# Top-k attention and two expert layers: cosine as a shifted sine, and max and min that read PSUM

## The chip, the core and the metric

The kernel runs on one core of a Trainium2 chip. The metric is the device time of one execution in microseconds (us). Five engines have a queue each and run side by side: PE (TensorE, matmuls into PSUM; its weight loads are shown as PEld), DVE (VectorE), ACT (ScalarE), POOL (GpSimd) and SP, which issues the DMAs. An engine takes its instructions in the order in which they were written; a wait stops everything behind it on that engine.

## What is computed

```python
scores = scale * q @ k.T            # 4 batches x 8 heads, 576 x 576, head size 64
kth    = the 32nd largest of each row
attn   = softmax over scores >= kth, others 0
x      = attn @ v                   # reshaped to 2304 tokens x 512
h      = x @ w_in                   # 512 -> 2048, w_in and w_out come as 64 bit floats
x      = (h * cos(h)) @ w_out       # back to 512
# then each token goes to the expert (of 8) with the largest logit:
y      = relu(x @ w1[e]) @ w2[e]    # 512 -> 1024 -> 512, times two gate factors
```

## The kernel before

Three pieces of work follow each other and overlap.

Attention runs in 80 units: 64 "m" units of 128 query rows of two heads, and 16 "x" units of the last 64 rows of two heads side by side. A unit transposes its queries on PE, makes scores of 128 x 288 per half row and head (L551, L566), and ACT copies each half from PSUM into the tile `sc` in SBUF (L557, L571). The two halves of a row are folded: DVE takes their elementwise maximum into `up` and their minimum into `dn` (L580). Four rounds of MAX8 (L590) with a MATCH_REPLACE8 between them (L595) take the 32 largest out of `up`; one MAX8 of `dn` (L585) and a last small one (L600) give the threshold and a flag by which a general path at the end recomputes all, if the fold was not enough. POOL makes small per-row values (L604 to L609), ACT a mask (L614), POOL subtracts it (L618), ACT takes the exponential and the row sums (L621), POOL and DVE the reciprocals (L624, L627). A DVE copy (L629) spreads the reciprocals over a 128 x 128 tile `rs`, which PE transposes (L653) beside the probabilities (L641, L652), so that after the product with v (L682) DVE can scale a transposed result (L688, L692).

The first expert layer ("MoE") works on chunks of 256 tokens as soon as their attention units are done, in 72 units of 256 hidden columns: 24 matmuls (L765 to L767), an ACT copy to `hs` (L771), then cos(h) as the sine of a folded angle: POOL makes r = h/2pi + 1/4 (L773), DVE rounds it to whole turns (L775), POOL subtracts these (L777), and ACT takes the sine, in groups of up to four units because a change between the tables of sine and exponential costs a load (L787). DVE multiplies (L795), ACT and POOL split the product in two parts (L806, L808), and 12 matmuls add it to the result (L816 to L818). Weights w_in and w_out are brought from 64 bits to two 32 bit parts in the first third (L714 to L750). Each chunk ends with its routing (L833 to L911).

The second expert layer, 8 experts, follows when all tokens are routed (L1028 to L1084).

The order on each engine is made when the program is written. A class `Plan` holds every step with a cost in ns for its engine and an urgency: ten per attention unit plus an offset per kind of step from the table `ADD`. It hands each engine the most urgent step that can start, and knows which of the limited buffers are free. Six of the eight PSUM banks (`ps`) serve all scores, transposes and MoE inputs in turn; the other two hold the sums of the first expert layer. There are four places for `sc`, four for `rr` (the angle), six for `hs` and one for `dn`. What waits for what on the chip is then set by the tiles' own readers and writers, in the order written. Two engines that read one PSUM bank are put one after the other as well, which the planner's steps don't count.

Of the kernel before, what the change touches and what calls it, by code (L numbers as in the profile page):

```python
# [8 lines left out]
F32 = mybir.dt.float32  # L9
# [8 lines left out]
P = 128  # L18
# [3 lines left out]
TWO_PI = 6.2831850  # L22
LOWEST = -3.0e38
# [5 lines left out]
UP_POOL = 0  # L29
ADD = {'q': -10.1,  # L30
 's': -13.9,
# [23 lines left out]
 'rs': 1,  # L55
# [13 lines left out]
class Buf:  # L69
    """A value in one of the places of its tag; the place is picked when the first op starts."""  # L70
# [16 lines left out]
class Plan:  # L87
    """Orders the ops of all engines: takes them in program order, finds what depends on what,
    and gives each engine the most urgent op that can start."""
# [9 lines left out]
    def tag(self, name, places, loose=False, under=None):  # L99
        """`places`: (ap, area, first, last) each; `under`: tags whose last values must have left the place."""  # L100
# [158 lines left out]
def pool(n):  # L259
    return 20.0 + n * 2.357  # L260
# [7 lines left out]
def tile_topk_attention_moe_moe2(ctx, tc, q, k, v, w_in, w_out, w_gate, w_ogate, w1, w2, out):  # L268
# [45 lines left out]
    ebias = const.tile([P, 2], F32, name="ebias")  # L314
    nc.gpsimd.memset(ebias[:, 0:1], float(-EXP_OFF * 2 ** 23))
    nc.gpsimd.memset(ebias[:, 1:2], float(2 ** 20))

# [19 lines left out]
    def x2_rows(j):  # L337
        kind, b, r = tiles[j]
        if kind == "m":
# [5 lines left out]
              + N["dn"] * HALF + N["bl"] * S + 9 * P + (N["qt"] + N["rs"] + N["xt"]) * P + 4 * (TOPK + 16) + 32  # L345
# [73 lines left out]
    cut.tag("rs", N["rs"], P)  # L419
# [6 lines left out]
    attn_tags = ("sc", "kt", "qr", "vr", "kr", "ptm", "ptx", "up", "dn", "bl", "qx", "vx", "kx", "qt", "rs", "xt", "mx",  # L426
# [24 lines left out]
    B_wg, B_table, B_x2d, B_seen, B_out = (plan.fixed() for _ in range(5))  # L451
# [74 lines left out]
    def attention(u):  # L526
# [18 lines left out]
        for c in range(2):  # L545
            if kind == "m":
                ps = [plan.buf("ps"), plan.buf("ps")]
                for j in range(2):
                    def mm(j=j, c=c, o=ps[j]):
                        at = (REM if j == 0 else 0) + c * HALF  # L550
                        nc.tensor.matmul(o.ap[:, 0:HALF], qt.ap[j * D:(j + 1) * D, :],  # L551
                                         kt.ap[j * D:(j + 1) * D, at:at + HALF], start=True, stop=True)

                    plan.op({"PE": 483.0}, mm, [qt, kt], [ps[j]], prio + ADD["s"], hold=[sc])
                for j in range(2):
                    plan.op({"ACT": act(HALF, psum=True)},
                            lambda j=j, c=c, o=ps[j]: nc.scalar.activation(  # L557
                                sc.ap[:, j, c * HALF:(c + 1) * HALF], o.ap[:, 0:HALF], AF.Copy),
                            [ps[j]], [(sc, j)], prio + ADD["s"])
            else:  # L560
                o = plan.buf("ps")

                def mm(c=c, o=o):
                    at = REM + c * HALF
                    for j in range(2):
                        nc.tensor.matmul(o.ap[j * D:(j + 1) * D, 0:HALF], qt.ap[j * D:(j + 1) * D, 0:REM],  # L566
                                         kt.ap[j * D:(j + 1) * D, at:at + HALF], start=True, stop=True)

                plan.op({"PE": 540.0}, mm, [qt, kt], [o], prio + ADD["s"], hold=[sc])
                plan.op({"ACT": act(HALF, psum=True)},  # L570
                        lambda c=c, o=o: nc.scalar.activation(sc.ap[:, 0, c * HALF:(c + 1) * HALF],  # L571
# [817 lines left out]
```

## Time and profile before

| what | value |
|---|---|
| time, median of 3 runs (lowest to highest) | 1383.35 us (1379.19 to 1383.68) |
| span of the profiled execution | 1382.2 us |
| DVE busy | 988.5 us (72%) |
| PE busy | 1180.1 us (85%) |
| POOL busy | 885.2 us (64%) |
| ACT busy | 854.9 us (62%) |
| last L580, the end of the attention's top-k work | begins at 965.1 us |

The profiled execution's span is 1.15 us below the median of the runs. Busy time is a share of the whole span; the stages differ, so the stretches below are 0 to 380 us (attention, weights being narrowed, few MoE units), 380 to 968 (attention and MoE together), 968 to 1045 (MoE alone), 1045 to 1075 (change to the second layer) and from 1075 on (second layer). [...]

### The profile page before, as it was taken

How to read it: one execution, taken by the hardware profiler on the slowest of the kernel's cores; microseconds unless marked ns; L12 is line 12 of the kernel's file. 1: busy time of each engine (PE TensorE's matmuls, PEld its weight loads, DVE VectorE, ACT ScalarE, POOL GpSimd, SP SyncE). 2: the span in 40 equal slices, each digit the busy share in tenths (PEclk: the TensorE clock that was granted, in tenths of full speed). 3: DMA queues.
4: the chain of work that ended last, by engine and by line, in shares of the span. 5: the costliest groups of instructions: out<-in, count | busy, mean ns of one | idle time of the engine just before them, and what ended most of it. 6: DMA issues, size and time to landing. Idle time of an engine off the chain costs nothing.

```text
span 1382.2 us, 22655 instructions
## 1 busy us (share of the span) xinstructions
PE 1180.1 (85%) x7478; PEld 936.6 (68%) x7479; DVE 988.5 (72%) x2864; ACT 854.9 (62%) x1854; POOL 885.2 (64%) x1130
## 2 busy tenths in 40 slices
PE   3467778768898999999989898899994599999996
PEld 2334555547677668668767676767883599999995
DVE  6999999779599888999987889888335234444410
ACT  5777777767577787777766668767555244444421
POOL 6778888888666865776676657766765455555400
PEclk9655779989999989999999999999996699999998
DMA  8223323534440343323345321241557444444100
GB/s 210 76 107 113 98 67 116 182 131 162 144 139 8 111 140 105 122 92 104 96 135 152 100 78 36 89 137 46 174 184 267 166 160 158 149 156 160 58 17 23
DMA packets 95807, 164.72 MB, mean 119 GB/s; under 512 B 49850, under 2 KB 54202, under 8 KB 95680
## 3 DMA queue, kind: packets, MB, share of 16 engines
q1 hardware_dynamic: 91264, 153.71, 34.3%
q0 software_dynamic: 4416, 9.47, 2.1%
q8 instruction: 61, 1.00, 0.3%
q14 instruction: 66, 0.54, 0.1%
HBM read 146.72 MB, written 19.56 MB: 120 GB/s over the span
## 4 chain that ended last, share of the span: by engine, by line
PE 41%; DVE 29%; POOL 13%; issue 10%; ACT 6%; DMA 2%; POOLq 0%; DVEq 0%; ACTq 0%
DVE area_a L590 7%; DVE area_a L595 6%; DVE area_a L580 6%; PE bank L682 4%; PE bank L551 3%; PE bank L816 3%; PE bank L818 3%; PE bank L817 3%; PE bank L1052 2%; PE bank L1053 2%; PE bank L641 2%; PE bank L1054 2%; POOL area_a L618 2%; PE bank L765 2%; POOL area_g L777 2%
## 5 line engine op out<-in xcount | busy, mean ns | idle before, releaser
L590 DVE MAX8 area_a<-area_a 128x8 f32<-128x288 f32 x576 | 243.6, 444 | 1.1
L618 POOL TENSOR_TENSOR area_a<-area_a 128x576 f32<-128x576 f32 x144 | 195.8, 1368 | 23.0 <-ACT area_a L614 21.9
L595 DVE MATCH_REPLACE8 area_a<-area_a 128x288 f32<-128x288 f32 x432 | 187.8, 438 | 0.0
L580 DVE TENSOR_TENSOR area_a<-area_a 128x288 f32<-128x288 f32 x288 | 176.7, 639 | 14.5 <-ACT area_a L557 11.0
L765 PE MATMUL bank<-area_f,area_w 128*128 128x256 f32 x576 | 177.6, 308 | 2.3 <-ACT area_h L771 2.3
L641 PE MATMUL bank<-ident,area_a 128*128 128x128 f32 x576 | 104.5, 313 | 70.6 <-ACT area_a L621 57.8
L766 PE MATMUL bank<-area_f,area_w 128*128 128x256 f32 x576 | 163.3, 284 | 0.0
L767 PE MATMUL bank<-area_f,area_w 128*128 128x256 f32 x576 | 163.0, 283 | 0.0
L551 PE MATMUL bank<-area_a 64*128 64x288 f32 x512 | 133.3, 513 | 25.5 <-ACT area_a L541 22.5
L641 PEld LDWEIGHTS bank<-ident,area_a 128*128 128x128 f32 x576 | 73.8, 158 | 100.3 <-ACT area_a L621 78.4
L816 PE MATMUL bank<-area_l,area_f 128*128 128x512 f32 x288 | 130.4, 453 | 1.3 <-ACT area_f L806 0.6
L614 ACT ACTIVATE area_a<-area_a 128x576 bf16<-128x576 f32 x144 | 107.3, 768 | 37.5 <-POOL area_a L604 37.2
L808 POOL TENSOR_TENSOR area_f<-area_g,area_f 128x256 fp32r<-128x256 f32 x144 | 114.9, 811 | 23.7 <-ACT area_f L806 20.8
L777 POOL TENSOR_TENSOR area_g<-area_g,area_n 128x512 f32<-128x512 f32 x72 | 105.7, 1468 | 35.3 <-DVE area_a L600 14.8
L621 ACT ACTIVATE area_a<-area_a 128x576 f32<-128x576 f32 x144 | 111.2, 773 | 27.1 <-POOL area_a L618 26.2
L682 PE MATMUL bank<-area_a 128*64 128x128 f32 (+3 forms) x1600 | 123.3, 296 | 1.5 <-ACT area_a L662 1.3
L818 PE MATMUL bank<-area_l,area_f 128*128 128x512 f32 x288 | 119.7, 416 | 5.3 <-POOL area_f L808 5.0
L765 PEld LDWEIGHTS bank<-area_f,area_w 128*128 128x128 f32 x576 | 112.1, 195 | 14.2 <-issue 9.2
L682 PEld LDWEIGHTS bank<-area_a 128*64 128x64 f32 (+1 forms) x1600 | 89.8, 150 | 42.3 <-issue 18.3
L817 PE MATMUL bank<-area_l,area_f 128*128 128x512 f32 x288 | 118.2, 410 | 0.0
L766 PEld LDWEIGHTS bank<-area_f,area_w 128*128 128x128 f32 x576 | 111.8, 194 | 1.0
L767 PEld LDWEIGHTS bank<-area_f,area_w 128*128 128x128 f32 x576 | 111.0, 193 | 0.0
(197 smaller groups left out, 3005.4 us busy)
## 6 DMA issues: line engine op xcount, KB each, us to landing
area_l<-wod SPq DMA_DIRECT2D x144, 512.0 KB, 3.6
area_l<-in_moe_w_dram SPq DMA_DIRECT2D x52, 512.0 KB, 4.3
area_l<-in_moe_w_in_dram SPq DMA_DIRECT2D x16, 512.0 KB, 4.3
area_l<-in_moe_w_out_dram SPq DMA_DIRECT2D x16, 512.0 KB, 4.1
wod<-area_l SPq DMA_DIRECT2D x16, 512.0 KB, 2.6
area_n<-in_moe_w_dram SPq DMA_DIRECT2D x12, 512.0 KB, 4.9
area_a<-in_k_dram SPq DMA_DIRECT2D x32, 128.0 KB, 3.5
area_a<-in_q_dram SPq DMA_DIRECT2D x32, 128.0 KB, 3.4
```

Source lines behind the costliest of these rows:

```text
L551: nc.tensor.matmul(o.ap[:, 0:HALF], qt.ap[j * D:(j + 1) * D, :], kt.ap[j * D:(j + 1) * D, at:at + HALF], start=True, stop=True)
L580: plan.op(cost, lambda j=j, to=to, op=op, eng=eng: eng.tensor_tensor(to(), sc.ap[:, j, 0:HALF], sc.ap[:, j, HALF:S], op=op), [(sc, j)], [( ...
L590: lambda j=j, t=t: nc.vector.max(mx.ap[:, j, 8 * t:8 * t + 8], up.ap[:, j, :]),
L595: lambda j=j, t=t: nc.vector.match_replace(up.ap[:, j, :], mx.ap[:, j, 8 * t:8 * t + 8], up.ap[:, j, :], LOWEST),
L618: plan.op({"POOL": 1234.0}, lambda j=j: nc.gpsimd.tensor_tensor(sc.ap[:, j, :], sc.ap[:, j, :], bl.ap[:, j, :], op=OP.subtract), [(bl, j)] ...
L641: nc.tensor.transpose(pp.ap[:, r_ * P:(r_ + 1) * P], flat[:, at + r_ * P:at + (r_ + 1) * P], ident)
L682: nc.tensor.matmul(o.ap[j * D:(j + 1) * D, 0:w], lh, rh, start=(r_ == 0), stop=(r_ == R))
L765: nc.tensor.matmul(o, w_in_h[:, c_, fs], xh[:, c_, :], start=(c_ == 0), stop=False)
L766: nc.tensor.matmul(o, w_in_h[:, c_, fs], xl[:, c_, :], start=False, stop=False)
L767: nc.tensor.matmul(o, w_in_l[:, c_, fs], xh[:, c_, :], start=False, stop=(c_ == KC - 1))
L816: nc.tensor.matmul(acc[t].ap, gh, wr(0), start=(f == 0), stop=False)
L818: nc.tensor.matmul(acc[t].ap, gl, wr(0), start=False, stop=(f == NF - 1))
```

## The change

The angle isn't folded any more. ACT takes sin(h + pi/2) straight from `hs`, with the quarter turn as a bias that it reads from a constant tile; the POOL step, the DVE step and the POOL step ahead of it (L773, L775, L777) are gone. So that the angle stays in the range of the sine, a guard bounds |h|: PE multiplies the token chunk and the weight columns with themselves (`gram`, 72 and 64 matmuls of 128 x 128), DVE takes the largest entry of each block (13 reductions), and at the end a token norm squared over 1.60 or a weight norm squared over 1.50 sends the program to the general path.

The first halves of the scores stay in PSUM for the maximum and the minimum: of each unit ACT copies the second half (`high`) to SBUF first, DVE reads the first half (`low`) from PSUM and the second from SBUF, and ACT copies `low` to `sc` as well, with an urgency of its own, for the later steps. The number of copies is the same. A `low` bank is free when DVE and ACT have both read it.

The spread of the reciprocal sums moves from DVE to PE: the copy L629 and the tile `rs` are gone, and instead of the transpose L653 PE multiplies the column of reciprocals, read with step 0 as 64 or 128 equal weight columns, with the identity (144 matmuls for 80 transposes).

```diff
         sc = plan.buf("sc")
...
+        low = [plan.buf("ps") for _ in range(n)]
+        high = [plan.buf("ps") for _ in range(n)]
...
+        plan.op({"PE": 620.0}, lambda: scores(1, high), [qt, kt], high, prio + ADD["s"], hold=[sc])
+        plan.op({"PE": 620.0}, lambda: scores(0, low), [qt, kt], low, prio + ADD["s"], hold=[sc])
+        for j in range(n):
+            plan.op({"ACT": act(HALF, psum=True)}, lambda j=j: nc.scalar.activation(
+                sc.ap[:, j, HALF:S], high[j].ap[:, 0:HALF], AF.Copy), [high[j]], [(sc, (j, 1))], prio + ADD["s"])
...
-                plan.op(cost, lambda j=j, to=to, op=op, eng=eng: eng.tensor_tensor(
-                    to(), sc.ap[:, j, 0:HALF], sc.ap[:, j, HALF:S], op=op),
-                    [(sc, j)], [(up, j) if o_ else dns[j]], prio + ADD["top"])
+                plan.op({"DVE": vec(HALF)}, lambda j=j, to=to, op=op: nc.vector.tensor_tensor(
+                    to(), low[j].ap[:, 0:HALF], sc.ap[:, j, HALF:S], op=op),
+                    [low[j], (sc, (j, 1))], [(up, j) if o_ else dns[j]], prio + ADD["top"])
...
+        for j in range(n):
+            plan.op({"ACT": act(HALF, psum=True)}, lambda j=j: nc.scalar.activation(
+                sc.ap[:, j, 0:HALF], low[j].ap[:, 0:HALF], AF.Copy), [low[j]], [(sc, (j, 0))], prio + ADD["low"])
...
-        plan.op({"DVE": 136.0}, lambda: nc.vector.tensor_copy(
-            rs.ap.rearrange("p (h d) -> p h d", h=n),
-            sm.ap[:, 6:6 + n, None].to_broadcast([P, n, P // n])), [(sm, 6)], [rs], prio + ADD["sum"])
...
-            nc.tensor.transpose(px.ap[:, P:2 * P], rs.ap, ident)
+            for j in range(n):
+                w_ = P // n
+                nc.tensor.matmul(px.ap[j * w_:(j + 1) * w_, P:2 * P], sm.ap[:, 6 + j:7 + j].to_broadcast([P, w_]), ident,
+                                 start=True, stop=True)
...
-        plan.op({"POOL": pool_s(512)}, lambda: nc.gpsimd.tensor_scalar(
-            rr.ap, hs.ap, INV_2PI, 0.25, op0=OP.mult, op1=OP.add), [hs], [rr], prio)
-        plan.op({"DVE": fast(512)}, lambda: nc.vector.tensor_scalar(
-            nn.ap, rr.ap, MAGIC, MAGIC, op0=OP.add, op1=OP.subtract), [rr], [nn], prio)
-        plan.op({"POOL": pool(512)}, lambda: nc.gpsimd.tensor_tensor(rr.ap, rr.ap, nn.ap, op=OP.subtract),
-                [nn], [rr], prio)
...
-                    nc.scalar.activation(x.ap, x.ap, AF.Sin, scale=TWO_PI)
+                for h_, x in zip(hss, rrs):
+                    nc.scalar.activation(x.ap, h_.ap, AF.Sin, bias=ebias[:, 2:3])
...
+    def gram(dst, n, cols, r, w, prio):
+
+        pg = plan.buf("ps")
...
+                    nc.tensor.matmul(pg.ap[:, i * P:(i + 1) * P], x, x, start=(c_ == 0), stop=(c_ == KC - 1))
...
+        plan.op({"DVE": vec(P * n, True)}, lambda: nc.vector.tensor_reduce(
+            dst, pg.ap[:, 0:P * n], axis=AX.X, op=OP.max), [pg], w, prio)
```

The planner makes a new order from these steps. Three places, before and after, show it. In the rows `bank_N` is a PSUM bank, `area_a` the attention's tiles in SBUF, `area_g` and `area_h` those of the angle and of h; the brackets name the engines that an instruction waits for. Line numbers after are those of the changed program: L572 is the maximum and minimum, L585 and L577 the MAX8, L590 the MATCH_REPLACE8, L622 the reciprocal, L683 the scaling, L557 the scores, L633 the transposes, L613 POOL's subtraction, L810 its split, L699, L599, L602 and L620 its small steps.

DVE before, about the middle of the attention, from the end of one unit's top-k to the start of the next:

```order
L775 TENSOR_SCALAR area_n<-area_g 128x512 [waits Pool_49]
L590 MAX area_a<-area_a 128x8 [waits DVE_49]
L627 RECIPROCAL area_a<-area_a 128x2 [waits Pool_49]
L595 MATCH_REPLACE area_a<-area_a 128x288 [waits DVE_49]
L629 COPY area_a<-area_a 128x128 [waits DVE_49]
L595 MATCH_REPLACE area_a<-area_a 128x288
L590 MAX area_a<-area_a 128x8 [waits DVE_49] x2
L600 MAX area_a<-area_a 128x8 [waits DVE_49]
L580 TENSOR_TENSOR area_a<-area_a 128x288 [waits Activation_49]
L600 MAX area_a<-area_a 128x8 [waits DVE_49]
L580 TENSOR_TENSOR area_a<-area_a 128x288
L580 TENSOR_TENSOR area_a<-area_a 128x288 [waits Activation_49]
```

DVE after, at a like place:

```order
L595 MAX area_a<-area_a 128x8 [waits DVE_49] x2
L683 TENSOR_TENSOR area_a<-bank_122,area_a 128x128 [waits PE_49,Activation_49]
L572 TENSOR_TENSOR area_a<-bank_118,area_a 128x288 [waits PE_49,Activation_49]
L572 TENSOR_TENSOR area_a<-bank_119,area_a 128x288 [waits PE_49,Activation_49]
L572 TENSOR_TENSOR area_a<-bank_118,area_a 128x288 [waits Activation_49]
L585 MAX area_a<-area_a 128x8 [waits DVE_49]
L577 MAX area_a<-area_a 128x8 [waits DVE_49]
L585 MAX area_a<-area_a 128x8
L572 TENSOR_TENSOR area_a<-bank_119,area_a 128x288 [waits DVE_49,Activation_49]
L590 MATCH_REPLACE area_a<-area_a 128x288
L577 MAX area_a<-area_a 128x8 [waits DVE_49]
L622 RECIPROCAL area_a<-area_a 128x2 [waits Pool_49]
```

The rounding L775 and the copy L629 are no longer there, and the first three of a unit's four maxima and minima name a bank; each of these waits for ACT, and the first of each bank for PE's matmul too.

PE before, the scores of one unit:

```order
L551 MATMUL bank_119<-area_a 128x288 [waits DVE_49]
L551 MATMUL bank_115<-area_a 128x288 [waits Activation_49]
L551 MATMUL bank_118<-area_a 128x288 [waits Activation_49]
L641 MATMUL bank_117<-ident,area_a 128x128 [waits Activation_49]
L641 MATMUL bank_117<-ident,area_a 128x128 x3
L551 MATMUL bank_116<-area_a 128x288
```

PE after, the scores of one unit:

```order
L557 MATMUL bank_122<-area_a 128x288 [waits Activation_49]
L557 MATMUL bank_121<-area_a 128x288
L557 MATMUL bank_117<-area_a 128x288 [waits DVE_49]
L557 MATMUL bank_120<-area_a 128x288 [waits DVE_49]
L818 MATMUL bank_123<-area_l_6081,area_f 128x512 [waits DMAHW0_49,Activation_49]
L819 MATMUL bank_123<-area_l_6081,area_f 128x512
L820 MATMUL bank_123<-area_l_6081,area_f 128x512 [waits Pool_49]
```

The two score matmuls of the first half, the second pair in the order, each wait for DVE to let go of a bank, and the matmuls of the MoE product (L818 and on) stand behind them. Of the 256 score matmuls of m units, 23 waited for DVE before and 74 do after.

POOL before, between the masks of two units:

```order
L618 TENSOR_TENSOR area_a<-area_a 128x576 [waits Activation_49]
L704 TENSOR_TENSOR area_f<-area_a,area_f 128x128 [waits Activation_49]
L618 TENSOR_TENSOR area_a<-area_a 128x576
L773 TENSOR_SCALAR area_g<-area_h 128x512 [waits Activation_49,Pool_49]
L624 TENSOR_SCALAR area_a<-area_a 128x2 [waits Activation_49]
L777 TENSOR_TENSOR area_g<-area_g,area_n 128x512 [waits DVE_49]
L604 TENSOR_SCALAR area_a<-area_a 128x2 [waits DVE_49]
```

POOL after:

```order
L613 TENSOR_TENSOR area_a<-area_a 128x576 [waits Activation_49]
L699 TENSOR_TENSOR area_f<-area_a,area_f 128x128 [waits Activation_49]
L613 TENSOR_TENSOR area_a<-area_a 128x576
L810 TENSOR_TENSOR area_f<-area_g,area_f 128x256 [waits PE_49,Activation_49,Pool_49]
L620 TENSOR_SCALAR area_a<-area_a 128x2 [waits Activation_49]
L599 TENSOR_SCALAR area_a<-area_a 128x2 [waits DVE_49]
L602 TENSOR_SCALAR area_a<-area_a 128x2
```

The two steps of the angle (L773, L777) are gone from between the subtractions and the small steps.

## Rows read from the trace of the kernel before

**Rows 1.** Stretches: us; busy (instructions) of PE, PEld, DVE, ACT, POOL; PE clock; DMA.

```profile
0.00:380.00 380.00, 267.77 (x1617) 190.30 (x1619) 325.69 (x886) 262.37 (x593) 294.11 (x372) 0.80 0.40 128
380.00:968.00 588.00, 546.43 (x3910) 419.73 (x3909) 521.06 (x1763) 430.18 (x1004) 395.98 (x566) 0.96 0.32 99
968.00:1045.00 77.00, 74.72 (x478) 63.66 (x476) 24.60 (x71) 39.06 (x79) 49.55 (x62) 1.00 0.60 198
1045.00:1075.00 30.00, 8.56 (x38) 7.63 (x38) 17.80 (x35) 17.32 (x20) 20.55 (x11) 0.53 0.70 248
1075.00:1382.00 307.00, 282.66 (x1440) 255.32 (x1440) 99.38 (x113) 105.97 (x161) 124.97 (x122) 0.96 0.33 114
```

**Rows 2.** Shares of the chain that ended last, stretches 0:380, 380:968 and 968:1045.

```profile
by line: DVE area_a L580 12.3%; DVE area_a L590 11.6%; DVE area_a L595 9.7%; PE bank L682 5.7%; issue 5.1%; DVE area_n L729 3.9%; DVE area_g L714 3.9%; DVE area_h L716 3.8%; DVE area_a L585 3.1%; POOL area_a L618 2.8%; DVE area_a L629 2.5%;
by line: DVE area_a L590 8.2%; DVE area_a L595 7.2%; PE bank L682 6.1%; PE bank L551 5.9%; DVE area_a L580 5.7%; PE bank L641 5.0%; PE bank L816 4.6%; PE bank L818 3.8%; PE bank L817 3.7%; issue 3.4%; POOL area_g L777 3.4%; POOL area_a L618
by line: PE bank L818 12.2%; PE bank L816 11.3%; PE bank L817 11.0%; PE bank L765 10.1%; PE bank L767 9.8%; PE bank L766 9.8%; DMA area_l<-in_moe_w_dram 6.9%; POOL area_g L777 3.8%; issue 3.2%; DVE area_a L595 2.2%; POOL area_f L808 2.2%; P
```

**Rows 3.** Groups by line: shapes xcount | busy us, mean ns | idle before, releasers.

```profile
L580 DVE TENSOR_TENSOR area_a<-area_a 128x288 f32<-128x288 f32 x288 | 176.7, 639 | 14.5 <-ACT area_a L557 11.0 <-ACT area_a L571 3.4
L557 ACT ACTIVATE area_a<-bank 128x288 f32<-128x288 f32 x256 | 93.0, 406 | 24.5 <-PE bank L551 23.3
L629 DVE COPY area_a<-area_a 128x128 f32<-128x128 f32 x80 | 33.8, 423 | 1.1 <-PE bank L653 0.9
L775 DVE TENSOR_SCALAR area_n<-area_g 128x512 f32<-128x512 f32 x72 | 33.1, 460 | 45.9 <-POOL area_g L773 45.8
L773 POOL TENSOR_SCALAR area_g<-area_h 128x512 f32<-128x512 f32 x72 | 47.4, 659 | 33.8 <-ACT area_h L771 29.1
L777 POOL TENSOR_TENSOR area_g<-area_g,area_n 128x512 f32<-128x512 f32 x72 | 105.7, 1468 | 35.3 <-DVE area_a L600 14.8 <-DVE area_n L775 8.9 <-DVE area_a L629 3.7
L653 PE MATMUL bank<-ident,area_a 128*128 128x128 f32 x80 | 26.2, 328 | 33.7 <-DVE area_a L629 33.5
L682 PE MATMUL bank<-area_a 128*64 128x128 f32 x1024 | 81.3, 309 | 0.0
L787 ACT ACTIVATE area_g<-area_g 128x512 f32<-128x512 f32 x72 | 39.9, 620 | 5.6 <-POOL area_g L777 5.3
L721 ACT ACTIVATE area_n<-area_l,ebias 128x512 f32<-128x512 uint32 x32 | 24.1, 757 | 1.3 <-POOL area_w L739 0.8 <-POOL area_g L777 0.5
```

**Rows 4.** Timeline at 606 us, DVE and POOL: start, us, instruction.

```profile
606.14 2.82 DVE L580 TENSOR_TENSOR area_a<-area_a 128x288 f32<-128x288 f32 x2 [0.45 <-ACT area_a L557]
605.89 2.75 POOL L618 TENSOR_TENSOR area_a<-area_a 128x576 f32<-128x576 f32 x2
```

**Rows 5.** One line's durations, ns min/median/max: two SBUF inputs, or one in PSUM.

```profile
L580 DVE TENSOR_TENSOR area_a<-area_a x288: 428/448/1557, 12.5 to 965.1; 128x288 f32<-128x288 f32 x144
L795 DVE TENSOR_TENSOR area_g<-area_h,area_g x72: 662/684/2187, 211.3 to 1036.5; 128x512 f32<-128x512 f32 x72
L688 DVE TENSOR_TENSOR area_a<-bank,area_a x64: 264/283/293, 41.7 to 982.2; 128x128 f32<-128x128 f32 x64
L1035 DVE TENSOR_TENSOR area_f<-bank,area_f x24: 680/691/693, 1085.8 to 1331.3; 128x512 fp32r<-128x512 f32 x24
```

**Rows 6.** DVE busy us (instructions) of L580 alone, in the first two stretches.

```profile
0.00:380.00 380.00, 69.29 (x93) 0.80 0.40 128
380.00:968.00 588.00, 107.42 (x196) 0.96 0.32 99
```

**Rows 7.** PE timeline at full clock: a pair of MoE matmuls, and four transposes.

```profile
1013.13 0.28 PE L765 MATMUL bank<-area_f,area_w 128*128 128x256 f32 x1
1013.25 0.28 PE L766 MATMUL bank<-area_f,area_w 128*128 128x256 f32 x1
...
568.57 0.60 PE L641 MATMUL bank<-ident,area_a 128*128 128x128 f32 x4
```

**Rows 8.** PE waiting for DVE, 0 to 968 us: us in total, times, longest.

```profile
PE bank L653 <- DVE area_a L629: 33.5, 27, 3.5
```

More of the change, by code (lines that the diff above doesn't have):

```diff
@@ L22 @@
 TWO_PI = 6.2831850
+HALF_PI = 1.5707963267948966
+X_LIMIT = 1.60
+W_LIMIT = 1.50
 LOWEST = -3.0e38
@@ L28 @@
 PATIENCE = {"PE": 1.0, "ACT": 1.0, "DVE": 1.0, "POOL": 1.0, "SP": 1.0}
-UP_POOL = 0
 ADD = {'q': -10.1,
+ 'low': 4.0,
  's': -13.9,
@@ L54 @@
  'qt': 2,
- 'rs': 1,
  'xt': 2,
@@ L449, in tile_topk_attention_moe_moe2 @@
     plan.tag("acc", banks[6:8])
-    B_wg, B_table, B_x2d, B_seen, B_out = (plan.fixed() for _ in range(5))
+    B_wg, B_table, B_x2d, B_seen, B_out, B_norms = (plan.fixed() for _ in range(6))
     B_wod = plan.fixed()
@@ L544, in attention @@
         sc = plan.buf("sc")
[L545 to L571, printed above, removed]
-                                                              o.ap[:, 0:HALF], AF.Copy),
-                        [o], [(sc, 0)], prio + ADD["s"])
@@ new lines, in attention, with scores @@
+        low = [plan.buf("ps") for _ in range(n)]
+        high = [plan.buf("ps") for _ in range(n)]
+        def scores(c, out):
+            at = REM + c * HALF
+            for j in range(2):
+                if kind == "m":
+                    lo = at if j == 0 else at - REM
+                    nc.tensor.matmul(out[j].ap[:, 0:HALF], qt.ap[j * D:(j + 1) * D, :],
+                                     kt.ap[j * D:(j + 1) * D, lo:lo + HALF], start=True, stop=True)
+                else:
+                    nc.tensor.matmul(out[0].ap[j * D:(j + 1) * D, 0:HALF], qt.ap[j * D:(j + 1) * D, 0:REM],
+                                     kt.ap[j * D:(j + 1) * D, at:at + HALF], start=True, stop=True)
@@ L757, in moe_unit @@
         xc = XC[c]
[L758 removed]
+        ph, hs, rr = plan.buf("ps"), plan.buf("hs"), plan.buf("rr")
         for i in range(2):
@@ L1108, in tile_topk_attention_moe_moe2 @@
         worst[:, 1:2], worst[:, 0:1], 0.0, float(CAP + 1), op0=OP.is_ge, op1=OP.mult), [], [B_worst], base)
+    plan.op({"DVE": 90.0}, lambda: nc.vector.tensor_reduce(worst[:, 2:4], norms, axis=AX.X, op=OP.max),
+            [B_norms], [B_worst], base)
+    for i, limit in ((2, X_LIMIT), (3, W_LIMIT)):
+        plan.op({"DVE": 80.0}, lambda i=i, limit=limit: nc.vector.tensor_scalar(
+            worst[:, i:i + 1], worst[:, i:i + 1], limit, float(CAP + 1), op0=OP.is_gt, op1=OP.mult),
+            [], [B_worst], base)
     def count():
         nc.tensor.matmul(pc.ap[:, 0:E], ones, seen, start=True, stop=True)
-        nc.tensor.matmul(pc.ap[:, E:E + 1], ones, worst[:, 1:2], start=True, stop=True)
+        for i in range(1, 4):
+            nc.tensor.matmul(pc.ap[:, E:E + 1], ones, worst[:, i:i + 1], start=(i == 1), stop=(i == 3))
     B_cnt = plan.fixed()
```

41 lines of the change are left out of this document (26 added, 15 removed).

## The prediction

> **What bounds the kernel now.** I read the busy times by stretch first [rows 1], then the chain of work that ended last in three of the stretches [rows 2], then the groups of instructions that the change touches [rows 3], and last the spread of single durations [rows 4, 5].
>
> From 0 to 380 us DVE is busy for 325.7 of 380 us (86%) and heads the chain with five of the first seven lines; the maximum and minimum, L580, has the largest share, 12.3%. PE is granted only 0.80 of its clock there, since it is idle often. From 380 to 968 us DVE is busy for 521 of 588 us (89%) and PE for 546 (93%), and the chain passes between them: L590, L595 and L580 of DVE hold 21.1%, PE's first six lines 29.1%. PE isn't at its rate there: two matmuls of 256 columns start 0.12 us apart, while each is 0.28 us long [rows 7]. From 968 to 1045 us the chain is PE's MoE work, and after 1045 us nothing that the change touches has a share. So the change can pay before 968 us, and there through DVE, then POOL, until PE or ACT is next.
>
> **What goes from DVE.** L580 takes 639 ns on the mean but 448 at the median and 428 at least [rows 3, 5]: a few are very long. Rows 4 show why. At 606 us two of them take 2.82 us, beside two subtractions of POOL that take 2.75 us and began 0.25 us earlier: an instruction of DVE with two inputs in SBUF waits while POOL reads SBUF. The two DVE lines with one input in PSUM have no such tail: L688 lies between 264 and 293 ns, L1035 between 680 and 693 [rows 5]. So the new instruction has a steady price. Between those lines' medians (283 ns at 128 elements, 691 at 512) a straight line gives 453 ns at 288. I take that, with 428 (the floor with both inputs in SBUF) and 639 (nothing won) as ends. DVE saves 288 x (639 - 453) = 54 us; the ends are 61 and 0.
>
> [...]
>
> The copy L629 (33.8 us) and the rounding L775 (33.1 us) go whole [rows 3]. The 13 new reductions cost at most what L1035 costs (691 ns, 9 us in all) and at least L688's 283 ns (4 us); I take 7. DVE's balance is 54 + 34 + 33 - 7 = 114 us of work less, nearly all of it before 968 us.
>
> **What goes from POOL.** L777 and L773, 105.7 + 47.4 = 153 us [rows 3]. Some of it was on the path; the rest frees POOL for the mask and the split, and collides with DVE less.
>
> **From work to time.** I price by the chain, line by line. 0 to 380: L580 has 12.3%, 46.7 us. Its 93 instructions took 69.3 us [rows 6] and would take 93 x 0.453 = 42.1, 39% less: 18.3 us. L629 has 2.5%: 9.5 us. 380 to 968: L580 has 5.7%, 33.5 us; 196 x 0.453 = 88.8 for 107.4 us, 17% less: 5.8 us. L777 has 3.4% there and 3.8% of the 77 us behind: 20.0 + 2.9 us. L773 and L775 don't stand among the first lines; at L777's rate of path to busy time, (47.4 + 33.1) / 105.7 x 22.9 = 17.4 us. L629 after 380 us likewise, at L580's rate, some 6 us. Sum: 18.3 + 9.5 + 5.8 + 22.9 + 17.4 + 6 = 80 us. A removed piece of the path is often followed by another that was nearly as late, so this is more than will be seen if nothing else speeds up; for the other side, if DVE kept its busy shares of 86 and 89%, 114 us of its work would be some 130 us of time.
>
> **What is added, and what it takes back.** (a) The 136 matmuls of the guard: four transposes of the same 128 columns take 0.60 us, about 0.11 each behind the first [rows 7]; 136 x 0.11 = 15 us, at most 136 x 0.328 (L653, which stands alone) = 45 us. Those of the weights, 64, fall into the first stretch, where PE is idle 30% of the time; the 72 of the tokens cost 8 us of PE, half of it on the path: 4 us. (b) The spread: 144 matmuls for 80 transposes. A full precision matmul leaves two records, 288 x 81.3 / 1024 = 23 us like L682, for 26.2 us of L653 removed [rows 3]: -3 us, or +21 if each of the 144 costs 0.328; I take +3. PE still waits there for DVE: L653 waited 33.5 us for the copy [rows 8], and the new matmul waits for the reciprocal just ahead of it. (c) The sine with a bias from a tile: ACT pays between L787's 620 and L721's 757 ns, 0 to 10 us over 72, off the path at ACT's 73%: 1 us. (d) The reductions and their waits: 3 us. (e) Two engines read each `low` bank one after the other. The order has 160 such banks, and in about 65 a maximum or minimum is written behind ACT's copy, 406 ns [rows 3]: 0 to 26 us on DVE, 10 taken because other DVE work stands between, half on the path: 5 us. (f) 51 more score matmuls wait for DVE to free a bank, with everything of PE behind them. The wait of PE for DVE's copy was 33.5 / 27 = 1.24 us each time that it showed [rows 8]: 0 to 63 us; I take 0.2 us each and half of that: 5 us. Together 21 us.
>
> Gain 80 - 21 = 59 us; with 153 of POOL's 690 us before 968 us gone, the long tail of DVE's other lines with two SBUF inputs shrinks too (L795 goes up to 2187 ns over a median of 684 [rows 5]): 5 us more. So 64 us off the profiled execution's span of 1382.2 us: 1318. The median of the runs lies 1.15 us over that span; I predict **1319 us**.
>
> **Rivals.** (1) DVE's whole saving becomes time, because PE has room: 0.12 us a matmul and the freed POOL let it follow, and its clock rises in the first stretch. Against it: PE is busy 93% from 380 us on, and 136 + 64 instructions are added. Price: 110 us, 1273 us. (2) The banks tie ACT, DVE and PE together more than I took: all of (e) and half of (f) on the path, 26 + 31 us for the 10 taken, leaves 64 - 47 = 17 us of gain, 1366 us. For it speaks that every maximum and minimum of the rows of the order waits for ACT or PE; against it, that DVE does them first in a unit, so that banks come free early. [...] (3) Slower. PE's scores wait for DVE, DVE's maxima for ACT, ACT's copies for PE's next scores; six banks hold two units' first halves, and PE stops with MoE products behind it. The 51 new waits at the longest wait on L629, 3.5 us [rows 8], would be 178 us; it decides from 64 + 5 over 51, 1.4 us each on the path. At 2 us each the time is 1382 - 69 + 102 = 1415, with the median's offset 1416 us. (4) It doesn't do what it says: the guard sends the inputs to the general path, which would cost far over the present time. With the reference's inputs the largest squared norms are 0.20 of 1.60 and 1.25 of 1.50, so I give it nothing. Or the new maximum still takes 639 ns: 24 us of path come back, 1343 us, which is inside the forecast's own range.
>
> **How the numbers follow.** Forecast 1319 (1290 to 1350): 0.60. Rival 1 (1250 to 1290): 0.13. Rival 2 (1350 to 1379): 0.15. Within 0.3% of 1383.35 us, 1379.2 to 1387.5, about what a measurement of this kernel can tell from no change: 0.05. Rival 3: 0.07. Faster is 0.60 + 0.13 + 0.15 = 0.88. The range leaves out rival 3, the no-change case and the lower half of rival 1 (0.19): 1270 to 1377 us.
>
> **What would show it.** Right: the maximum and minimum at 430 to 480 ns with no tail over 600; DVE's busy time down by 100 to 120 us; POOL's by about 150; the last maximum at 895 to 910 us instead of 965; the stretch behind it unchanged. Wrong: PE waits for a maximum or minimum over 30 us in all (rivals 2, 3); the reciprocal still holding PE for 30 us; DVE waits for ACT's copies of `low` that outgrow 15 us; or a last top-k before 870 us (rival 1).

## The result and the profile after

The changed kernel takes 1316.05 us (median of 4 runs, 1313.37 to 1318.61), beside 1381.27 us for the kernel before on the same chip: a ratio of 0.9528, 95% interval 0.9507 to 0.9548. That is 4.7% or 65 us less; the prediction was 1319 us. Its profiled execution has a span of 1315.2 us.

The first line of the page after, busy time by engine:

```profile
PE 1177.5 (90%) x7826; PEld 953.0 (72%) x7827; DVE 879.7 (67%) x2728; ACT 853.9 (65%) x1852; POOL 684.9 (52%) x988
```

DVE lost 108.8 us, within the 100 to 120 that the prediction named. POOL lost 200.3 us where the removed lines had 153, and the prediction had named about 150: 47 us went that nobody removed (experiment 2 shows from where most of them came). PE's busy time is nearly the same as before.

The stretches: the first cut is at 380 us as in [rows 1], the later ones are at the same events; the 30 us of the change to the second layer are left out. Columns: busy time (instructions) of PE, PEld, DVE, ACT, POOL, then granted clock, DMA share, GB/s:

```profile
0.00:380.00 380.00, 304.41 (x1996) 225.71 (x1998) 313.80 (x973) 287.98 (x652) 264.90 (x376) 0.86 0.46 142
380.00:905.00 525.00, 505.30 (x3847) 398.55 (x3846) 428.57 (x1550) 405.89 (x945) 247.59 (x441) 0.97 0.34 102
905.00:980.00 75.00, 73.25 (x491) 64.01 (x490) 25.11 (x62) 41.63 (x81) 34.53 (x43) 1.00 0.65 214
1010.00:1315.00 305.00, 281.29 (x1440) 253.41 (x1440) 97.37 (x112) 104.84 (x160) 121.91 (x121) 0.95 0.33 109
```

The stretch that was 380 to 968 now ends at about 905, so the gain lies before that point: the last maximum began at 965.1 us and now begins at 901.3, 63.8 us earlier. What follows it is as long as before, 414 us for 417. In the second stretch PE is busy 96% of the time (93% before) and DVE 82% (89% before): DVE has become the one that waits.

The groups that answer to [rows 3]: the maximum and minimum (L572, before L580), the multiply behind the sine (L797, before L795), ACT's copy of the first halves (L580), the sine (L776, before L787), the spread (L647, in place of L653), POOL's subtraction (L613, before L618). Columns: count, busy us, mean ns, idle time of the engine just before them and what ended it:

```profile
L572 DVE TENSOR_TENSOR area_a<-bank,area_a 128x288 f32<-128x288 f32 x288 | 121.1, 445 | 40.4 <-PE bank L557 13.9 <-PE bank L560 8.8 <-ACT area_a L566 8.0
L797 DVE TENSOR_TENSOR area_g<-area_h,area_g 128x512 f32<-128x512 f32 x72 | 55.0, 790 | 15.7 <-ACT area_g L776 15.6
L580 ACT ACTIVATE area_a<-bank 128x288 f32<-128x288 f32 x144 | 54.8, 411 | 11.7 <-DVE area_a L572 7.4 <-PE bank L557 4.2
L776 ACT ACTIVATE area_g<-area_h,ebias 128x512 f32<-128x512 f32 x72 | 46.3, 712 | 0.2
L647 PE MATMUL bank<-ident,area_a 128*64 128x128 f32 (+1 forms) x288 | 38.4, 326 | 2.0 <-DVE area_a L622 1.9
L613 POOL TENSOR_TENSOR area_a<-area_a 128x576 f32<-128x576 f32 x144 | 186.7, 1305 | 37.7 <-ACT area_a L609 37.6
```

L572 takes 445 ns for 639; all four maxima and minima of a unit read a bank, not only the first three of the order shown above. DVE's idle time in front of it rose from 14.5 us [rows 3] to 40.4, more than half of it for PE's scores (L557, L560). All its instructions, minimum, median and maximum in ns, with the start of the first and the last in us; and those of the matmuls of the guard (L790):

```profile
L572 DVE TENSOR_TENSOR area_a<-bank,area_a x288: 426/446/459, 11.7 to 901.3; 128x288 f32<-128x288 f32 x144
L790 PE MATMUL bank<-area_f x72: 223/280/476, 143.0 to 927.4; 128*128 128x128 f32 x72
L790 PE MATMUL bank<-area_w x64: 272/415/477, 32.0 to 208.9; 128*128 128x128 f32 x64
```

The longest maximum has gone from 1557 ns [rows 5] to 459.

### The profile page after: what moved, and what is told of

It reads as the page before. It is cut to its first block, busy times and chain, and to the rows that moved or that the text cites. A ratio compares the mean times of both kernels' runs of the same rounds, so it can differ in the third digit from the quotient of the medians.

```text
span 1315.2 us, 23122 instructions
## 1 busy us (share of the span) xinstructions
PE 1177.5 (90%) x7826; PEld 953.0 (72%) x7827; DVE 879.7 (67%) x2728; ACT 853.9 (65%) x1852; POOL 684.9 (52%) x988
## 5 line engine op out<-in xcount | busy, mean ns | idle before, releaser
L585 DVE MAX8 area_a<-area_a 128x8 f32<-128x288 f32 x576 | 243.1, 447 | 1.4
L613 POOL TENSOR_TENSOR area_a<-area_a 128x576 f32<-128x576 f32 x144 | 186.7, 1305 | 37.7 <-ACT area_a L609 37.6
L590 DVE MATCH_REPLACE8 area_a<-area_a 128x288 f32<-128x288 f32 x432 | 188.7, 441 | 0.1
L810 POOL TENSOR_TENSOR area_f<-area_g,area_f 128x256 fp32r<-128x256 f32 x144 | 108.2, 767 | 85.4 <-ACT area_f L808 54.9
L572 DVE TENSOR_TENSOR area_a<-bank,area_a 128x288 f32<-128x288 f32 x288 | 121.1, 445 | 40.4 <-PE bank L557 13.9
L633 PE MATMUL bank<-ident,area_a 128*128 128x128 f32 x576 | 98.0, 301 | 47.3 <-ACT area_a L566 20.9
L818 PE MATMUL bank<-area_l,area_f 128*128 128x512 f32 x288 | 128.1, 445 | 1.3 <-DMA area_l<-wod 1.3
L760 PEld LDWEIGHTS bank<-area_f,area_w 128*128 128x128 f32 x576 | 110.3, 191 | 20.3 <-issue 12.7
L633 PEld LDWEIGHTS bank<-ident,area_a 128*128 128x128 f32 x576 | 72.3, 153 | 66.6 <-ACT area_a L566 25.7
L557 PE MATMUL bank<-area_a 64*128 64x288 f32 x512 | 103.4, 473 | 16.4 <-ACT area_a L545 10.8
L820 PE MATMUL bank<-area_l,area_f 128*128 128x512 f32 x288 | 115.1, 400 | 1.1 <-POOL area_f L810 1.0
L819 PE MATMUL bank<-area_l,area_f 128*128 128x512 f32 x288 | 116.0, 403 | 0.0
L616 ACT ACTIVATE area_a<-area_a 128x576 f32<-128x576 f32 x144 | 111.4, 774 | 6.8 <-POOL area_a L613 6.2
L761 PEld LDWEIGHTS bank<-area_f,area_w 128*128 128x128 f32 x576 | 110.8, 192 | 1.2
L636 ACT ACTIVATE area_a<-bank 128x512 f32<-128x512 f32 x144 | 85.2, 596 | 39.1 <-PE bank L633 35.8
L762 PEld LDWEIGHTS bank<-area_f,area_w 128*128 128x128 f32 x576 | 110.0, 191 | 0.0
```

The source lines that it names most:

```text
L572: plan.op({"DVE": vec(HALF)}, lambda j=j, to=to, op=op: nc.vector.tensor_tensor(to(), low[j].ap[:, 0:HALF], sc.ap[:, j, HALF:S], op=op), [ ...
L585: lambda j=j, t=t: nc.vector.max(mx.ap[:, j, 8 * t:8 * t + 8], up.ap[:, j, :]),
L590: lambda j=j, t=t: nc.vector.match_replace(up.ap[:, j, :], mx.ap[:, j, 8 * t:8 * t + 8], up.ap[:, j, :], LOWEST),
L613: plan.op({"POOL": 1234.0}, lambda j=j: nc.gpsimd.tensor_tensor(sc.ap[:, j, :], sc.ap[:, j, :], bl.ap[:, j, :], op=OP.subtract), [(bl, j)] ...
L633: nc.tensor.transpose(pp.ap[:, r_ * P:(r_ + 1) * P], flat[:, at + r_ * P:at + (r_ + 1) * P], ident)
L760: nc.tensor.matmul(o, w_in_h[:, c_, fs], xh[:, c_, :], start=(c_ == 0), stop=False)
```

## The experiments

Each comparison is the ratio to the kernel before in runs on the same chip, with its 95% interval; 1% of the kernel before is 13.8 us, and sums below are made of ratios, so a difference of two kernels is good to some 4 to 6 us. "Its order" means the order of instructions on every engine, which the planner makes anew for every change of the steps or their costs.

**1. One part at a time.** Three kernels, each the kernel before with one part of the diff above and nothing else. The maximum and minimum, with the order of scores and copies that belongs to it:

```diff
-                    to(), sc.ap[:, j, 0:HALF], sc.ap[:, j, HALF:S], op=op),
+                    to(), low[j].ap[:, 0:HALF], sc.ap[:, j, HALF:S], op=op),
```

> The kernel before with max and min that read the first half of the scores in PSUM, and the new order of copies, alone. Theory A: 18.3 + 5.8 us less 5 for waits on copies and 5 for scores that wait for DVE: 14 us of gain, 1367 us, 0.990. Rival B (0.57 of the 54 us of DVE work): 31 us, 1350 us, 0.978. Rival C (POOL counted): DVE's mean goes down to 453 ns all the same, but the time by under 8 us. In A and B the 288 instructions lie at 430 to 480 ns.

Measured: 0.9512 (0.9486 to 0.9537), 67 us of gain, as much as the whole change and over twice what any theory gave it. The sine with its guard:

```diff
-                    nc.scalar.activation(x.ap, x.ap, AF.Sin, scale=TWO_PI)
+                    nc.scalar.activation(x.ap, h_.ap, AF.Sin, bias=ebias[:, 2:3])
```

> The kernel before with the shifted sine and its guard alone; max, min and spread as before. Theory A (the prediction's chain, line by line): the three lines of the fold give 22.9 + 17.4 us and up to 5 us for fewer meetings with POOL, the sine's bias, the guard and its reductions take back 8: 32 to 37 us of gain, about 1346 us, ratio 0.974. Rival B (each us taken from DVE is worth the same, 65 us of gain over 114 us of DVE work, 0.57): DVE loses 33 and gets 7, so 15 us of gain, 1366 us, 0.989. Rival C (POOL was the one that counted; the rest of DVE gets shorter by itself): 45 us or more, under 1336 us.

Measured: 0.9811 (0.9787 to 0.9835), 26 us, between A and B. The spread:

```diff
-            nc.tensor.transpose(px.ap[:, P:2 * P], rs.ap, ident)
+            for j in range(n):
+                w_ = P // n
+                nc.tensor.matmul(px.ap[j * w_:(j + 1) * w_, P:2 * P], sm.ap[:, 6 + j:7 + j].to_broadcast([P, w_]), ident,
+                                 start=True, stop=True)
```

> The kernel before with the reciprocal sums spread by TensorE alone. Theory A: 9.5 + 6 us less 3 for PE: 12.5 us of gain, 1369 us, 0.991. Rival B (0.57 of 33.8 us): 19 us, 1362 us, 0.986. Rival C: the copy was late only because of the work ahead of it, so under 6 us. If the three parts add up, their gains make 65 us together; a sum of 80 or more means that they buy the same wait twice, one under 50 that they need each other.

Measured: 1.0064 (1.0041 to 1.0088), 9 us slower: no theory had that sign. The three sum to 85 us for the 65 of the whole, so they don't add up, and one of them is a loss.

**2. Why the maximum is worth so much: its source or its order.** The kernel with the new maximum alone, its order kept on every engine, with the first half taken from an SBUF place (where older scores lie, so that the results are of no use):

```diff
-                    to(), low[j].ap[:, 0:HALF], sc.ap[:, j, HALF:S], op=op),
+                    to(), sc.ap[:, j, (HALF if u < 6 else 0):(S if u < 6 else HALF)], sc.ap[:, j, HALF:S], op=op),
```

> The kernel with only the new max and min, in exactly its order on every engine, but DVE takes the first half from the place of the scores in SBUF as the unit before left it, not from PSUM; the results are of no use, and the two tests that start the general path are left out. It parts the source from the order. Rival D (the source): 288 instructions go back to about 639 ns, 57 us of DVE work return, and with 68 us of gain for them the time is 1360 us or more. Rival E (the order: two copies of ACT ahead of the first maximum and not four, scores as one piece on PE): the instructions get longer as well, but only the 24 us of path that the prediction gave them come back, 1334 us or less. In both, if the tail comes from two SBUF sources beside POOL, single ones go over 1 us.

Measured: 0.982 (0.9787 to 0.9854), where PSUM had 0.9512. That is 1357 us, 3 short of what D named and far from E's 1334. With the order held, the source alone is 3.1%, some 43 us; the other 25 us are the order's. The line, first from PSUM, then from SBUF:

```profile
L568 DVE TENSOR_TENSOR area_a<-bank,area_a 128x288 f32<-128x288 f32 x288 | 119.7, 442 | 8.0 <-ACT area_a L576 2.7 <-PE bank L553 2.1 <-PE bank L556 1.3
L568 DVE TENSOR_TENSOR area_a<-bank,area_a x288: 426/441/459, 11.7 to 890.7; 128x288 f32<-128x288 f32 x144
```

```profile
L568 DVE TENSOR_TENSOR area_a<-area_a 128x288 f32<-128x288 f32 x288 | 170.6, 618 | 4.7 <-ACT area_a L562 2.7 <-ACT area_a L576 1.6
L568 DVE TENSOR_TENSOR area_a<-area_a x288: 428/447/1555, 11.1 to 940.2; 128x288 f32<-128x288 f32 x144
```

The same instructions in the same places: the median differs by 6 ns (second row of each: minimum, median, maximum) and the mean by 176. Two lines of the timeline of the SBUF kernel (start and length in us) show one of the long ones, begun 0.09 us after a subtraction of POOL and ended 0.32 us after that was through (608.40 for 608.08):

```profile
606.79 1.29 POOL L609 TENSOR_TENSOR area_a<-area_a 128x576 f32<-128x576 f32 x1 [0.36 <-ACT area_a L605]
606.88 1.52 DVE L568 TENSOR_TENSOR area_a<-area_a 128x288 f32<-128x288 f32 x1
```

With both inputs in SBUF the longest maximum takes 1555 ns, with one in PSUM 459, beside the same instructions of POOL. The busy lines of the two kernels, PSUM first, add that it works both ways:

```profile
PE 1139.3 (87%) x7478; PEld 917.5 (70%) x7479; DVE 943.1 (72%) x2864; ACT 850.5 (65%) x1854; POOL 841.8 (64%) x1130
```

```profile
PE 1153.6 (85%) x7478; PEld 921.8 (68%) x7479; DVE 993.2 (73%) x2864; ACT 850.7 (63%) x1854; POOL 880.5 (65%) x1130
```

POOL runs the same 1130 instructions in 38.7 us less when DVE reads PSUM. Against the kernel before it is 43.4 us less (841.8 for 885.2), most of the 47 that nobody had removed. The 43 us of time therefore hold two things, 50.9 us less of DVE's work and 38.7 us less of POOL's; this run can't part them.

**3. Which part of the order.** The kernel before with the scores as one piece per half, second half first, but all four copies of ACT ahead of a maximum that reads SBUF:

```diff
+        for j in range(n):
+            plan.op({"ACT": act(HALF, psum=True)}, lambda j=j: nc.scalar.activation(
+                sc.ap[:, j, 0:HALF], low[j].ap[:, 0:HALF], AF.Copy), [low[j]], [(sc, (j, 0))], prio + ADD["s"])
         mx, up, dns = plan.buf("mx"), plan.buf("up"), [plan.buf("dn") for _ in range(n)]
```

> The kernel before with the new order of the scores alone: a half of both heads as one piece on PE, second half first, but all four copies of ACT come ahead of max and min, which read both halves in SBUF. The run with the old halves in SBUF gained 1.8% with the same instructions on DVE, from the order alone. Rival K (the two copies that went behind the top-k made that gain): nothing left here, 0.995 to 1.005. Rival L (scores as one piece made it): 0.980 to 0.988.

Measured: 0.9911 (0.989 to 0.9933), between K and L: 12 of the 25 us come with the scores as one piece, 13 with the two copies that no longer stand ahead of the first maximum. The planner made an order of its own for each of these kernels, so what a new order brings by chance is in both figures and isn't parted from them. The wait of PE that got shorter is that for the exponential, so for a unit's top-k to be done. Here it is (us in all, times, longest) in the kernel before, then with the scores as one piece, then with two copies behind as well, then with PSUM as well:

```profile
PE bank L641 <- ACT area_a L621: 57.8, 44, 7.1
```

```profile
PE bank L633 <- ACT area_a L612: 61.8, 38, 7.1
```

```profile
PE bank L633 <- ACT area_a L612: 35.3, 29, 7.0
```

```profile
PE bank L633 <- ACT area_a L612: 20.5, 11, 6.3
```

A unit's probabilities come earlier for it, first by the copies and then by the source. What the scores as one piece gave is not in this wait (61.8 us for 57.8), and I have no row for it.

**4. What the changed kernel is without its spread, its guard, or both.** Without the guard (the matmuls and reductions of `gram` and the test are gone), without the spread (copy and transpose put back), and with neither:

> The changed kernel without the guard: the 136 matmuls of the norms and the 13 reductions are left out, and so is the test for too large an angle. Theory A: the guard costs 4 + 3 us, so 1309 us. Rival B: it lies wholly beside other work, 1316 us, no difference beyond 0.3%. Rival C: it is dearer, since a block needs a bank and PE waits for its operands: 15 us or more, under 1301 us.

> The changed kernel with DVE's copy of the reciprocals and the transpose put back, max, sine and guard as they are. Theory F (the 144 matmuls cost PE 24 us where it is the bound, and the copy's time on DVE comes back as longer instructions of its other lines anyway): 10 to 25 us faster than the changed kernel, 1291 to 1306 us. Theory A (DVE's 33.8 us count): slower, 1325 to 1331 us.

> The changed kernel with neither the guard (left out with its test for too large an angle) nor the spread: the new max and min, and the shifted sine. If the guard's 22.6 us and the spread's 10.8 us add up: 1283 us. If both are paid only because PE is the bound, and PE has room without them: 1270 us or less. If the spread helps once the max is shorter: 1295 us or more.

| the new maximum and the sine, and | ratio to before | 95% interval | median us |
|---|---|---|---|
| guard and spread (the change) | 0.9528 | 0.9507 to 0.9548 | 1316.05 |
| spread, no guard | 0.9384 | 0.9361 to 0.9408 | 1293.46 |
| guard, no spread | 0.9363 | 0.9336 to 0.9391 | 1292.91 |
| neither | 0.9339 | 0.9311 to 0.9368 | 1288.99 |

The spread costs 23 us beside the guard and 6 without it; the guard costs 20 us beside the spread (theory C of the run without the guard) and 3 without it, and these 3 can't be told from nothing by the intervals. Theory F holds: the spread is a loss. The kernel with neither, 1289 us, lies between what was expected of it if the two costs add up (1283) and if the spread helps (1295). **The version with guard and no spread computes all that the change does, and at 1292.91 us it beats both kernels**, the change by 23 us.

**5. Is it PE's time or the planner's order?** Two kernels in exactly the order of the change, with less work on PE. First the spread, one matmul per unit for two:

```diff
-            for j in range(n):
-                w_ = P // n
-                nc.tensor.matmul(px.ap[j * w_:(j + 1) * w_, P:2 * P], sm.ap[:, 6 + j:7 + j].to_broadcast([P, w_]), ident,
-                                 start=True, stop=True)
+            nc.tensor.matmul(px.ap[:, P:2 * P],
+                             sm.ap[:, 6:7].to_broadcast([P, P]),
+                             ident,
+                             start=True, stop=True)
```

> The changed kernel in exactly its order, but the spread of a unit of two heads is one matmul with the first head's reciprocal for both: 64 of 144 matmuls are left out, the second head's scale with them, and so is the test for a full expert. Theory F (PE's time counts): 128 records of 288 at 0.06 to 0.1 us from start to start are 8 to 13 us of PE, nearly all on the path: 1303 to 1308 us, ratio to the kernel before 0.944 to 0.948. Rival I (the work hides; what the spread costs lies in the order that the planner makes with it): within 4 us of the changed kernel, 1312 us or more.

Measured: 0.9438 (0.9416 to 0.9459), 12 us less than the change for 64 matmuls, 0.19 us each. Then the guard, a quarter of its matmuls:

```diff
-                for c_, x in enumerate(cols(i)):
-                    nc.tensor.matmul(pg.ap[:, i * P:(i + 1) * P], x, x, start=(c_ == 0), stop=(c_ == KC - 1))
+                for x in cols(i)[:1]:
+                    nc.tensor.matmul(pg.ap[:, i * P:(i + 1) * P], x, x, start=True, stop=True)
```

> The changed kernel in exactly its order, but of each norm only a quarter is summed: 102 of the 136 matmuls of the guard are left out, its 13 reductions and all its waits stay. Theory F (PE's time counts): 102 x 0.18 us from start to start are 18 us of PE at the most, 12 to 18 of them on the path: 1298 to 1304 us, ratio 0.940 to 0.945. Rival I (the order, the banks and the waits cost, the matmuls don't): 1312 us or more.

Measured: 0.9455 (0.9432 to 0.9478), 10 us for 102 matmuls, 0.10 us each. Rival I falls in both, and F is met within 0.001, a little past its edge for the spread and a little short of it for the guard: with the order held, most of what PE is spared is time. PE's busy time fell by 17.7 us (1159.8 for 1177.5) and 15.8 us (1161.7), the time by 12 and 10.

At these prices PE's work is 12 us of the 23 that the spread costs beside the guard (64 matmuls more than the 80 transposes that it replaces, taking one of either as equally dear), and 136 x 0.10 = 14 us of the guard's 20 beside the spread. The rest isn't shown. A candidate is a wait that the order with both parts has: PE's transposes stand behind ACT's copy of a second half (L566; L568 without the spread), which frees a bank. In the changed kernel, with one spread matmul a unit, without the spread, and without the guard:

```profile
PE bank L633 <- ACT area_a L566: 20.9, 11, 9.3
```

```profile
PE bank L633 <- ACT area_a L566: 19.3, 10, 9.4
```

```profile
PE bank L639 <- ACT area_a L568: 7.9, 3, 6.3
```

```profile
PE bank L633 <- ACT area_a L566: 5.9, 5, 1.7
```

It is 13 to 15 us longer with both, and stays when PE has less to do. But other waits differ as well (that of the same transposes for the exponential, L616, is 15.1 us in the changed kernel and 22.1 without the guard), so no cause is shown by it. PE's and DVE's busy times in the kernels without the spread (with guard, then with neither) are these:

```profile
PE 1162.7 (90%) x7618; PEld 941.0 (73%) x7619; DVE 898.6 (70%) x2808; ACT 853.9 (66%) x1852; POOL 685.8 (53%) x988
```

```profile
PE 1136.5 (88%) x7478; PEld 920.3 (72%) x7479; DVE 888.0 (69%) x2792; ACT 855.1 (67%) x1854; POOL 686.0 (53%) x988
```

Guard and spread together are 41 us of PE on top of the last line (1177.5 - 1136.5), and 26 us of time. Why the guard's 26 us of PE cost only 3 us once the spread is gone is open: the planner makes another order for it, and no kernel here holds that order.

**6. DVE's copy and the fold, priced in the order of before.** The copy of the reciprocals, cut to 2 columns a head:

```diff
-            rs.ap.rearrange("p (h d) -> p h d", h=n),
-            sm.ap[:, 6:6 + n, None].to_broadcast([P, n, P // n])), [(sm, 6)], [rs], prio + ADD["sum"])
+            rs.ap.rearrange("p (h d) -> p h d", h=n)[:, :, 0:(P // n if u < 2 else 2)],
+            sm.ap[:, 6:6 + n, None].to_broadcast([P, n, P // n if u < 2 else 2])), [(sm, 6)], [rs], prio + ADD["sum"])
```

> The kernel before in exactly its order, with DVE's copy of the reciprocals cut to 2 of 64 (or 128) columns a head from the third unit on, so later units are scaled with old values; the test for a full expert is left out. It prices DVE's copy with no work added on PE. Theory A (the chain): 9.5 + 6 us of gain, ratio 0.989. Rival J (the time comes back as longer instructions of DVE's other lines and a wait for the reciprocal): 5 us or less, 0.996 or more.

Measured: 0.9995 (0.9981 to 1.0008), nothing, as rival J had it. But the cut hardly shortened the copy, so it doesn't price it. The copy, with 128 columns before, then with 4 or 2:

```profile
L629 DVE COPY area_a<-area_a x80: 199/219/1285, 37.3 to 979.0; 128x128 f32<-128x128 f32 x80
```

```profile
L629 DVE COPY area_a<-area_a x80: 145/170/1260, 37.3 to 967.9; 128x4 f32<-128x4 f32 x62, 128x2 f32<-128x2 f32 x16, 128x128 f32<-128x128 f32 x2
L629 DVE COPY area_a<-area_a 128x4 f32<-128x4 f32 (+2 forms) x80 | 31.7, 396 | 1.1 <-PE bank L653 1.0
```

With a 32nd of its columns it is busy for 31.7 us instead of 33.8. With all columns its median is 219 ns and its mean 423: about half of its time is not the copy's but a wait of the kind in experiment 2 (in the kernel before, 24 of the 27 copies over 0.4 us end 0.07 to 0.11 us after an instruction of POOL), and a short copy waits as long. One of 4 columns, begun 0.03 us after POOL's subtraction L777 and ended 0.03 us after that was through:

```profile
606.42 1.26 POOL L777 TENSOR_TENSOR area_g<-area_g,area_n 128x512 f32<-128x512 f32 x1
606.45 1.26 DVE L629 COPY area_a<-area_a 128x4 f32<-128x4 f32 x1
```

So this run leaves open what the copy's removal alone is worth; it shows that its 33.8 us were not work that could be removed by having less of it.

The fold, its three instructions cut to 8 of 512 columns:

```diff
-            rr.ap, hs.ap, INV_2PI, 0.25, op0=OP.mult, op1=OP.add), [hs], [rr], prio)
+            rr.ap[:, 0:8], hs.ap[:, 0:8], INV_2PI, 0.25, op0=OP.mult, op1=OP.add), [hs], [rr], prio)
```

> The kernel before in exactly its order, with the fold's three instructions cut to 8 of 512 columns and the sine taken of h itself with the quarter turn as its bias; no guard. It prices POOL's 140 us and DVE's 28 us at an unchanged order. Theory A (the chain): 22.9 + 17.4 + 5 - 1 = 44 us of gain, 1334 us, ratio 0.968. Theory G: the 26.5 us that the sine alone gained, with the 22.6 us of the guard given back, 49 us, 1329 us. Rival H: the guard is cheap while PE still waits, so the fold is worth 30 us or less, 1348 us or more.

Measured: 0.9731 (0.9703 to 0.976), 37 us, between A and H. The maximum gets shorter by it, 607 ns for 639 [rows 3], beside a POOL that is busy for 762.0 us instead of 885.2:

```profile
L581 DVE TENSOR_TENSOR area_a<-area_a 128x288 f32<-128x288 f32 x288 | 167.3, 607 | 15.9 <-ACT area_a L558 9.6 <-ACT area_a L572 5.4 <-issue 0.8
```

Behind the new maximum, which has no such wait left (459 ns at most in experiment 2), the sine is worth less: from 0.9512 to 0.9339 without guard, 24 us.

## Why the prediction was right, and which of its steps were not

The time was met (1319 against 1316 us), the place of the gain too, and the sum of 64 us; but the sum held by luck, because errors of both signs cancelled: a gain of 67 us where 14 were given, against a loss of 23 where a gain of 12.5 was. Put one behind the other, the parts were worth (each from the two ratios named above; they sum to the whole by their making, and with the spread put ahead of the guard the last two would be -6 and -20):

| part | predicted | measured |
|---|---|---|
| maximum from PSUM, with its order, (e) and (f) | 24.1 - 10 = 14 us | 67 us |
| fold gone, sine with bias, fewer meetings with POOL | 22.9 + 17.4 - 1 + 5 = 44 us | 24 us behind the maximum (37 in the order of before, without it) |
| guard, (a) and (d) | -7 us | -3 us |
| spread, copy gone | 15.5 - 3 = 12.5 us | -23 us |
| sum | 64 us | 65 us |

- **The maximum's duration** was right: 453 ns forecast, 445 measured, with no tail (459 at most). The median is 446 ns from PSUM, and 447 from SBUF in experiment 2.
- **What that is worth was mis-sized.** The step took L580's share of the chain, 24.1 us for 54 us of DVE work. In an order held fixed, 50.9 us of DVE work (170.6 - 119.7) made some 43 us of time. The share of one chain counts an instruction only where that chain runs through it. DVE was 89% busy and PE waited for the units' probabilities; POOL's 38.7 us came with the saving, where the sum had 5 us for fewer meetings, and what each of the two gave isn't parted.
- **(e) and (f) had the wrong sign.** I priced the reordering by the waits that it adds: 10 us of loss. The waits were even smaller than taken: PE waited 2.4, 1.3 and 0.7 us for L572, DVE 6.4 us for ACT's copies of `low`, and ACT 7.4 us for L572. But the reordering itself was worth 25 us of gain, for which the sum had no term. As far as experiment 3 parts it, two copies of ACT, 0.41 us each, no longer stand between the scores and the first maximum, and the scores come in one piece. That rows 8 showed PE waiting 33.5 us for DVE's copy, at the end of the same path from scores to probabilities, could have told me.
- **The spread was wrong on both sides.** The 33.8 us of L629 were counted as work; about half were waits for POOL (mean 423 ns, median 219). In the kernel with the spread alone DVE's busy time fell by only 6.6 us (981.9 for 988.5), as other lines took up the waits: of L775's successor the mean went from 460 ns [rows 3] to 533. And (b) was priced at +3 us, next to the -3 of busy time counted from overlapping records (two matmuls 0.12 us apart, each 0.28 us long [rows 7]), though its own upper end, +21 us, was written beside it; at 0.19 us for each of the 64 matmuls more, PE paid 12; the cause of the other 11 is open (experiment 5).

```profile
L772 DVE TENSOR_SCALAR area_n<-area_g 128x512 f32<-128x512 f32 x72 | 38.4, 533 | 57.6 <-POOL area_g L770 57.2
L649 PE MATMUL bank<-ident,area_a 128*64 128x128 f32 (+1 forms) x288 | 39.6, 334 | 18.8 <-DVE area_a L624 18.4
```

  PE's wait didn't go either in that kernel: from 33.5 us for the copy [rows 8] to 18.4 for the reciprocal ahead of it. In the changed kernel it is down to 1.9, but most of that isn't the spread's doing: with the copy still there, the kernel with the new maximum alone has 16.7, and the one with the sine and its guard as well 5.7.
- **The guard** at 0.11 us a matmul was well sized (0.10 measured), but the claim that most of it hides was not: beside the spread it cost 20 us. The weights' share was supposed to fall where PE is idle; with three quarters of the guard's matmuls gone, the 40th of the 144 last MAX8s ends 7.4 us earlier (280.7 for 288.1 us), and all of the weights' matmuls lie ahead of that point (the last at 208.9 us). Without the spread the guard cost 3 us, under the 7 that I gave it.
- **The sine** takes 712 ns, between the 620 and 757 named. DVE waits 15.6 us for it in front of the multiply L797 (4.3 us before, L795); what the bias costs in time was not tried by itself.
- **Rivals.** Rival 1 was half right: more of the saving becomes time where PE has less added to it, 1289 us in the kernel with neither guard nor spread; that PE's 96% in the changed kernel is what stopped it is argued, and shown only for the 12 and 10 us of experiment 5. Rivals 2 and 3 fell in the terms that they priced: the waits for maxima and for copies of `low` are the few us above. The wait of experiment 5 for copies of the second half, 20.9 us, is also one at a bank; no term of (e) or (f) had it. Rival 4 fell as well.

## What to carry to other kernels

Where the mean of a DVE instruction lies far over its median, as here (639 ns for 448 [rows 3, 5]), the difference can be a wait, not work: before counting it as removable, look for what it meets in the timeline, ask what will take up the wait, and whether a source in PSUM removes its cause, as it did here (459 ns at most for 1557). The share of one chain can be far too low a price: here it was 24 us where the source alone gave 43, while for the fold it was near (44 us for 37). So test it with a kernel that holds the order, and look for what a reordering takes off the path from input to the first dependent step, not only for the waits that it adds. Moving small work to TensorE is no gift: here PE was busy for 80% and 96% of the two stretches that matter, and about two thirds of the busy time of the matmuls left out in experiment 5 came back as time.

## What the runs showed of the hardware that was not expected

- DVE and POOL lengthened each other's instructions: with DVE's 288 maxima on PSUM instead of SBUF, order held, these took 119.7 us for 170.6, and POOL's unchanged 1130 instructions 841.8 us for 880.5.
- A DVE copy of 4 or 2 columns took 396 ns on the mean and 1260 at most, nearly as much as one of 128 columns (423 and 1285), though the medians are 170 and 219: the one shown in experiment 6 took 1.26 us, as long as POOL's subtraction beside it.
- A maximum from PSUM was no slower than one from SBUF at the median: 446 ns (441 in the order of experiment 2) against 447, at 288 elements.
